# Attention with the AV product turned round, whole heads batched, and a fixed order of instructions across heads

## Chip, cores, metric

One Trainium2 chip, one of its cores. The metric is the device time of one execution in microseconds. Before: 785.48 us (median of 15 runs, 783.91 to 795.9).

## The reference, cut

```python
# attention: q, k, v are [8, 12, 448, 64]
scores = matmul(q, k.T) / sqrt(64)
m = max(scores, -1);  e = exp(scores - m)
attn = e / (sum(e, -1) + exp(-m) + 1e-9)      # "softmax off by one": exp(s) / (sum(exp(s)) + 1)
x = matmul(attn, v)                           # -> x[3584, 768], heads side by side
# soft mixture of experts on x: logits x @ phi, softmax over tokens, slot inputs d.T @ x,
# 8 experts of two layers (3 MB of weights a layer), and c @ slot_out -> [3584, 768]
```

## The kernel before

Only the attention loop matters here. There are 96 heads; a head is 448 rows, in four blocks of 112. "Scores" are q x k, `ex` their exponentials, and "AV" is the product of `ex` and v. PE is the matmul engine, DVE the vector engine, ACT the scalar engine, POOL the GpSimd engine; PSUM is the memory that matmuls write, SBUF the one that they read. Of a matmul's two operands the stationary one is loaded into PE's array first, as weights (LDWEIGHTS in the traces, counted as PEld: 2856 of them to 2857 matmuls from 10 to 580 us), and the matmul then reads the moving one.

```python
for j in range(NJ):                                     # NJ = 4
    tq = qkT_psum.tile([D, SC], BF16, tag="t")          # 112x64 -> 64x112, on PE
    nc.tensor.transpose(tq, qb[:, j, :], ident[0:SC, 0:SC])
    nc.vector.tensor_copy(qT[:, j * SC:(j + 1) * SC], tq)
    ...                                                 # the same for k
for j in range(NJ):
    sc = sc_psum.tile([SC, S], F32)
    nc.tensor.matmul(sc, kT[:, j * SC:(j + 1) * SC], qT, start=True, stop=True)
    nc.scalar.activation(ex[:, j, :], sc, AF.Exp, scale=scale)
for i in range(NJ):
    av = av_psum.tile([SC, D + 1], F32, tag="av")       # rows: queries; last column: denominator
    for j in range(NJ):
        nc.tensor.matmul(av, ex[:, j, i * SC:(i + 1) * SC], vb[:, j, :], ...)
    nc.vector.tensor_scalar_add(den, av[:, D:D + 1], 1.0)
    nc.vector.reciprocal(rec, den)                      # 112x1: one element per partition
    nc.vector.tensor_scalar_mul(x_sb[:, t, h * D:(h + 1) * D], av[:, 0:D], rec)
if h % 2 == 1: ...                                      # four transposes x -> xT, four ACT copies
```

A scheduler orders the instructions on each engine.

The softmax here doesn't subtract the row's maximum and nothing guards it: scores larger than these inputs give would overflow.

## Time and profile before

| | before |
|---|---|
| median of 15 runs | 785.48 us |
| attention | up to about 580 us |
| logits and slot inputs | 580 to 611 us |
| expert weights, output | 611 to 784 us |
| one head, from score to score | 5.94 us |
| PE's changes of array shape | 11.9 a head |

A matmul uses a part of PE's array, rows x columns: scores 64x112, the old AV 112x112 (64*112 and 112*112 in the traces). For the count both numbers are rounded up to 32, 64 or 128, so 112x112, 112x128 and 112x65 all count as the whole array; a change of shape is a matmul that uses another part than the one before it. The rounding is a convention of this text; the traces agree with it in two places: from AV (112x112) to a back transpose (112x128) starts are 93 ns apart, and 94 from AV to AV; in the changed kernel the same pair (112x65, then 128x112) is 373 ns apart, and AV to AV 374.

A matmul's duration in the trace is its latency, and neighbours overlap (four old AV matmuls of about 0.29 us each take 0.58 us together): to see what PE issues, read the distance from one start to the next. The prediction below shows these lines. One line of the page needs a warning, PE's granted clock in 40 slices of the run:

```profile
PEclk9999999999999999999999999999999687677855
```

It says full clock throughout attention. The matmuls say half clock: where the trace does record the clock, those of 512 columns in the weights' stage (L217) take 631 ns and start 427 ns apart at a granted clock of 0.50, and take 379 and start 216 apart at 1.00 (medians); attention's scores, of 448 columns, start 373 ns apart, which is 427 x 448/512. "Cold" below means half clock. The trace's list of clock changes begins only at 587 us, and the row is filled with the full clock up to the first change. Before the first change, trust the durations.

### The profile page before, as it was taken

The numbers are of one execution on the slowest core, as the hardware profiler recorded it, in microseconds if no ns is written. First come the engines' busy times: TensorE is split into PE (matmuls) and PEld (weight loads), VectorE is DVE, ScalarE is ACT, GpSimd is POOL, SyncE is SP. The second block draws the span as 40 slices with busy tenths as digits, with TensorE's granted clock in tenths as the row PEclk, the third lists the DMA queues.
The fourth block names the chain that finished last, engine by engine and source line by source line (L and its number), as shares of the span: only waits on it lengthen the run. The fifth ranks groups of instructions, "written<-read, shape, count | busy, mean of one in ns | idle before, by whom it ended". The sixth has DMA issues, their size and how long they took to land. (4 is left out here: it accounts for less than half of the span.)

```text
span 783.7 us, 11334 instructions
## 1 busy us (share of the span) xinstructions
PE 684.8 (87%) x3376; PEld 377.4 (48%) x3376; DVE 387.7 (49%) x2078; ACT 282.2 (36%) x731; POOL 167.9 (21%) x437
## 2 busy tenths in 40 slices
PE   5999999999999999999999999999998466676674
PEld 2555555555555555555555555555544122222221
DVE  2555555554555555555545555555540233443597
ACT  2444334434334443344343344333433142332200
POOL 3221222121212212221212222122100144342300
PEclk9999999999999999999999999999999687677855
DMA  4221121212111212212121112111000899999387
GB/s 134 60 66 54 59 64 55 60 54 65 60 54 54 65 54 60 65 53 60 54 66 60 54 54 66 54 59 54 7 1 1 329 432 427 433 424 434 123 283 253
DMA packets 44109, 95.20 MB, mean 121 GB/s; under 512 B 6160, under 2 KB 38416, under 8 KB 42000
## 3 DMA queue, kind: packets, MB, share of 16 engines
q1 hardware_dynamic: 44048, 94.49, 33.9%
q8 instruction: 26, 0.43, 0.2%
q14 instruction: 35, 0.29, 0.1%
HBM read 83.46 MB, written 11.01 MB: 121 GB/s over the span
## 5 line engine op out<-in xcount | busy, mean ns | idle before, releaser
L100 ACT ACTIVATE ex<-sc 112x448 bf16<-112x448 f32 x384 | 196.0, 544 | 155.5 <-PE sc L97 155.5
L105 PEld LDWEIGHTS <-ex 112*112 112x112 bf16 x1536 | 179.1, 200 | 129.8 <-DVE x_sb L116 62.0
L105 PE MATMUL av<-vb,ex 112*112 112x65 bf16 x1536 | 238.4, 287 | 0.8
L97 PE MATMUL sc<-qT,kT 64*112 64x448 bf16 x384 | 194.7, 595 | 4.9 <-DVE qT L85 4.9
L113 DVE TENSOR_SCALAR den<-av 112x1 f32<-112x1 f32 x384 | 57.7, 158 | 143.7 <-PE av L105 140.6
L84 PE MATMUL tq<-ident,qb 112*64 112x112 bf16 x384 | 113.3, 295 | 17.5 <-DVE qT L85 14.2
L85 DVE COPY qT<-tq 64x112 bf16<-64x112 bf16 x384 | 78.5, 204 | 87.1 <-PE tq L84 80.1
L129 ACT COPY xT_sb<-tp 128x112 bf16<-128x112 bf16 x192 | 48.4, 252 | 196.5 <-PE tp L125 192.8
L87 PE MATMUL tk<-ident,kb 112*64 112x112 bf16 x384 | 114.2, 297 | 5.2 <-DVE kT L88 4.9
L116 DVE TENSOR_SCALAR x_sb<-av,rec 112x64 bf16<-112x64 f32 x384 | 102.0, 275 | 2.7
L88 DVE COPY kT<-tk 64x112 bf16<-64x112 bf16 x384 | 76.4, 199 | 41.6 <-PE tk L87 38.1
L78 POOL CAST qb<-qf 112x256 bf16<-112x256 f32 x96 | 38.0, 396 | 238.4 <-issue 232.3
L91 POOL CAST vb<-vf 112x256 bf16<-112x256 f32 x96 | 38.7, 403 | 204.3 <-issue 94.8
L97 PEld LDWEIGHTS <-kT 64*112 64x112 bf16 x384 | 61.8, 183 | 37.6 <-issue 11.6
L84 PEld LDWEIGHTS <-qb 112*64 112x64 bf16 x384 | 51.2, 137 | 54.5 <-POOL kb L79 15.3
L87 PEld LDWEIGHTS <-kb 112*64 112x64 bf16 x384 | 54.3, 143 | 25.1 <-POOL vb L92 8.5
L217 PE MATMUL hp<-w1t,siT 128*4 128x512 bf16 x96 | 34.6, 515 | 29.4 <-ACT w1t L212 15.2
L114 DVE RECIPROCAL rec<-den 112x1 f32<-112x1 f32 x384 | 53.5, 148 | 1.0
L125 PE MATMUL tp<-ident,x_sb 112*128 112x112 bf16 x192 | 53.7, 280 | 0.0
L245 PE MATMUL sop<-w2t,hTt 128*32 128x384 bf16 x128 | 36.9, 458 | 6.4 <-ACT w2t L241 4.5
L212 DVE CAST w1t<-w1f 128x1024 bf16<-128x1024 f32 x16 | 18.0, 1170 | 45.4 <-DMA w1f<-in_moe_w_dram 45.4
L79 POOL CAST kb<-kf 112x256 bf16<-112x256 f32 x96 | 38.4, 400 | 5.8 <-PE tk L87 3.6
(50 smaller groups left out, 340.6 us busy)
## 6 DMA issues: line engine op xcount, KB each, us to landing
w1f<-in_moe_w_dram SPq DMA_DIRECT2D x8, 3072.0 KB, 26.0
w2f<-in_moe_w_dram SPq DMA_DIRECT2D x8, 3072.0 KB, 26.2
qf<-in_q_dram SPq DMA_DIRECT2D x96, 112.0 KB, 2.0
kf<-in_k_dram SPq DMA_DIRECT2D x96, 112.0 KB, 2.1
vf<-in_v_dram SPq DMA_DIRECT2D x96, 112.0 KB, 2.0
out_dram<-ot SPq DMA_DIRECT2D x32, 336.0 KB, 3.5
phi_f<-in_moe_phi_dram SPq DMA_DIRECT2D x1, 96.0 KB, 2.6
```

The source lines that it names most:

```text
L84: nc.tensor.transpose(tq, qb[:, j, :], ident[0:SC, 0:SC])
L85: nc.vector.tensor_copy(qT[:, j * SC:(j + 1) * SC], tq)
L87: nc.tensor.transpose(tk, kb[:, j, :], ident[0:SC, 0:SC])
L88: nc.vector.tensor_copy(kT[:, j * SC:(j + 1) * SC], tk)
L97: nc.tensor.matmul(sc, kT[:, j * SC:(j + 1) * SC], qT, start=True, stop=True)
L100: nc.scalar.activation(ex[:, j, :], sc, AF.Exp, scale=scale)
L105: nc.tensor.matmul(av, ex[:, j, i * SC:(i + 1) * SC], vb[:, j, :], start=(j == 0), stop=(j == NJ - 1),)
L113: nc.vector.tensor_scalar_add(den, av[:, D:D + 1], 1.0)
L114: nc.vector.reciprocal(rec, den)
L116: nc.vector.tensor_scalar_mul(x_sb[:, t, h * D:(h + 1) * D], av[:, 0:D], rec)
L125: nc.tensor.transpose(tp, x_sb[:, t, fb * 128:(fb + 1) * 128], ident[0:SC, 0:SC],)
L129: nc.scalar.copy(xT_sb[:, fb, t * SC:(t + 1) * SC], tp)
```

## The change

The intent: AV with v as the stationary operand, so four wide matmuls replace sixteen narrow ones and the result is born transposed; copies and normalisation for a whole head at once; and a software pipeline over heads in an order fixed by hand on PE, DVE, ACT and POOL. The diff, cut to its core (left out: the back transposes, now from xT to x with one copy for four, an unused constant that goes, and the layout of lines):

```diff
+            for src, dst in ((qb, qT), (kb, kT)):
+                tt = qkT_psum.tile([D, S], BF16, tag="t")
+                for j in range(NJ):
+                    nc.tensor.transpose(tt[:, j * SC:(j + 1) * SC], src[:, j, :], ident[0:SC, 0:SC])
+                nc.vector.tensor_copy(dst, tt)
...
-                    av = av_psum.tile([SC, D + 1], F32, tag="av")
-                        nc.tensor.matmul(av, ex[:, j, i * SC:(i + 1) * SC], vb[:, j, :], ...)
-                    nc.vector.tensor_scalar_add(den, av[:, D:D + 1], 1.0)
-                    nc.vector.reciprocal(rec, den)
-                    nc.vector.tensor_scalar_mul(x_sb[:, t, h * D:(h + 1) * D], av[:, 0:D], rec)
+            av = av_psum.tile([D + 1, S], F32)
+            for j in range(NJ):
+                nc.tensor.matmul(av, vb[:, j, :], ex[:, j, :], ...)
+            nc.scalar.add(den1, av[D:D + 1, :], 1.0)             # 1x448, one partition
+            nc.vector.reciprocal(rec1, den1)
+            nc.gpsimd.partition_broadcast(recb, rec1)            # 64x448
+            nc.vector.tensor_mul(xT_sb[...], av[0:D, :], recb)
...
+        with tc.manual_schedule(engines={PE, DVE, Activation, Pool}):
+            load(0)
+            for n in range(NH + 3):
+                qkT(n); load(n + 1); mul(n - 3); recip(n - 2); scores(n); av_mm(n - 1); xtr(n - 3)
```

## The prediction

> **What bounds the kernel now.** I read the views from coarse to fine: the stretches by stage, the costliest groups, the waits, one tile, then single instructions in time. The stretches first (columns: start:end us, length, then busy us and instruction count of each engine, granted TensorE clock, DMA share, GB/s):
>
> ```profile
> 10.00:580.00 570.00, 549.84 (x2857) 322.29 (x2856) 296.67 (x1901) 231.38 (x572) 113.57 (x372) 1.00 0.19 56
> 580.00:594.00 14.00, 14.00 (x59) 5.41 (x59) 2.62 (x14) 4.98 (x16) 0.00 (x0) 1.00 0.00 1
> 594.00:611.00 17.00, 14.27 (x97) 7.77 (x96) 0.84 (x4) 4.34 (x34) 0.00 (x0) 1.00 0.00 1
> 611.00:738.00 127.00, 78.94 (x293) 32.87 (x294) 47.42 (x56) 40.24 (x108) 48.97 (x43) 0.73 0.93 397
> 738.00:783.60 45.60, 25.97 (x67) 7.96 (x65) 38.38 (x98) 0.00 (x0) 0.00 (x0) 0.57 0.75 242
> ```
>
> Attention (96 heads) takes the first 580 us; logits, slot inputs, expert weights (DMA share 0.93) and output take the last 204. The change rewrites attention alone, where PE is the busiest engine: 549.84 of 570. The score tile gives the pace of a head:
>
> ```profile
> L97 PE MATMUL sc<-qT,kT x384: 526/619/619, 10.1 to 578.5; 64*112 64x448 bf16 x192
> ```
>
> From 10.1 to 578.5 us there are 95.75 heads: 5.94 us each. What PE does in it is in the groups:
>
> ```profile
> L105 PE MATMUL av<-vb,ex 112*112 112x65 bf16 x1536 | 238.4, 287 | 0.8
> L97 PE MATMUL sc<-qT,kT 64*112 64x448 bf16 x384 | 194.7, 595 | 4.9 <-DVE qT L85 4.9
> ...
> L84 PE MATMUL tq<-ident,qb 112*64 112x112 bf16 x384 | 113.3, 295 | 17.5 <-DVE qT L85 14.2
> ...
> L87 PE MATMUL tk<-ident,kb 112*64 112x112 bf16 x384 | 114.2, 297 | 5.2 <-DVE kT L88 4.9
> ...
> L125 PE MATMUL tp<-ident,x_sb 112*128 112x112 bf16 x192 | 53.7, 280 | 0.0
> ```
>
> The means are latencies of overlapping matmuls, so I take start-to-start times from the timeline:
>
> ```profile
> 301.49 1.28 PE L97 MATMUL sc<-qT,kT 64*112 64x448 bf16 x3 [0.21 <-DVE qT L85]
> 302.70 0.58 PE L105 MATMUL av<-vb,ex 112*112 112x65 bf16 x4
> 303.21 0.30 PE L84 MATMUL tq<-ident,qb 112*64 112x112 bf16 x1
> 303.31 0.30 PE L87 MATMUL tk<-ident,kb 112*64 112x112 bf16 x1
> 303.54 0.58 PE L105 MATMUL av<-vb,ex 112*112 112x65 bf16 x4
> ```
>
> Four av matmuls in 0.58 us, the last lasting 0.29, are 97 ns apart; over the trace the median is 94 ns, that of sc to sc 373 ns, and of tq to tk 95 ns. But between kinds PE loses time: av to tq is 212 ns, tk to av 230, sc to av 507, each 115 to 135 above the same pair without a change of array shape (av to tp, both over the full array, loses nothing). The scheduler interleaves the kinds so finely that PE changes shape 11.9 times a head (counted in PE's order in the trace). So one head is 4 x 373 + 16 x 94 + 8 x 94 + 2 x 94 = 3.9 us of issue, some 1.5 us of shape changes and 0.5 us of waits. PE's "busy" hides the switches.
>
> [...] For sc's 448 columns[...] the trace has 526 to 619, and 373 ns apart[...]. So attention runs cold from end to end, although the stretches print a clock of 1.00. The logits matmuls, N = 512,[...] 609 ns before 587 us, 379 after. [...] The trace cannot say: every reciprocal in it has one element per partition (148 ns). [...]
>
> **The change, part by part, per head.**
> AV is turned round: v is stationary and ex streams, 4 matmuls of 448 columns in place of 16 of 65. Cold, 4 x 373 = 1.49 us instead of 16 x 94 = 1.50. The swap itself saves PE nothing; 12 weight loads leave, which were hidden or equal.
> The transposes of q and k stay 8 (0.75 us). Back transposes stay 4 per two heads, now 128 columns (107 ns, 0.21 us a head).
> The order is fixed by hand: 8 transposes, 4 scores, 4 AV of the head before, back transposes. Shape changes fall from 11.9 to 3: about 0.38 us instead of 1.5.
> But a wait comes in: scores follow the transposes with nothing between. From the start of the last transpose 0.34 us to the copy's start (300.24 to 300.58 in the timeline), 0.38 us of copy, 0.05 to the first score: 0.77 us, of which 0.22 would be there anyway.
> PE's loop from one first score to the next, cold: three scores 1.12, the fourth held by the first exp to 1.22; score to AV 0.51; AV 3 x 0.373 = 1.12; AV to transposes 0.49; 7 x 0.093 = 0.65; wait 0.77. Sum 4.76 us, and 5.19 on the odd heads with four back transposes (0.43).
>
> DVE. Eight copies of 112 columns (8 x 0.20) and twelve small operations (4 x (158+148+275) = 2.32 us) leave. In come two copies of 448 ([...]0.38 us each, 0.35 start to start), a multiply of 448 from PSUM with an SBUF factor ([...]0.59 us, sized on the output's 384-column scalings, 0.52 us apart), and one reciprocal of 1 x 448 on a single partition: [...]3.8 us[...]. Sum 0.70 + 0.59 + 3.8 = 5.09 us. The order on DVE in the built program is copy, copy, multiply, reciprocal, repeated.
>
> ACT: 4 exps (434 ns apart, 1.74), one add of 448 (0.45), half a copy of 512 (0.3): 2.5 us. POOL: casts and memset 0.40 x 3 + 0.11 = 1.3, broadcast 0.6 to 0.9[...]: about 2.1 us. Neither binds.
>
> Both long loops share the copies: they wait for the transposes and for the reciprocal. So a head costs the larger of the two: 5.1 to 5.15 on even heads, 5.2 to 5.25 on odd ones. I take **5.2 us**. The multiply waits for the broadcast of the reciprocal that has just ended (0.6 to 0.9 us plus handover), while the two copies take 0.7, so that adds little or nothing.
>
> Sum: first score near 9 us, as now; 95.3 x 5.2 = 496, last score at 505. Then the pipeline drains: three heads' multiplies and two further reciprocals in series, each with broadcast and multiply: 3 + 2 x 5.2 + 2 = 15 us, so logits begin at about 520 instead of 580. They are no longer interleaved with attention's end: some 12 us instead of 14. The rest is untouched. 60 + 2 = 62 us off the profiled 785.5 gives 723; the plain runs spread from 786.7 to 795.9, so I add a little: **725 us**.
>
> **The rivals.**
> A. The reciprocal streams[...] (0.6 us). Then DVE needs 1.9 us and PE's cold loop rules: 4.98 a head, and a shorter drain: about 700 us.
> B. As A, and the denser matmuls wake the clock: scores and AV 190 ns apart, PE's loop near 3.3 us: 550 to 580 us. For it: PE's loop is 77% matmuls against 66%, in longer runs. Against: it needs A; with the slow reciprocal a warm PE only waits for DVE at 5.1.
> C. The broadcast is slow, 1.5 to 2 us[...]. Then reciprocal, broadcast, multiply chain on DVE without cover: 3.8 + 1.7 + 0.15 + 0.6 = 6.2 us a head, no better than 5.94: 780 to 810. For it: nothing in the profile prices it.[...]
> D. The gain is hidden by the weight transfers. Against: they start only when slot inputs are done (first weight transfer at 611 us, tied to the end of si), so they move forward as a block.
>
> **Range and chances.** The slow reciprocal (85%) with a short broadcast gives 700 to 745, depending on whether handovers add 0.2 us a head (20 us). Rival A or B 10%, C 5%. Range 702 to 750. Faster by over 2% 0.93, same 0.04, slower 0.03.
>
> **What would show each step.** Right: RECIPROCAL of 1x448 at 3.7 to 3.95 us, DVE over 90% busy in attention, sc to sc one head apart 5.1 to 5.3 us, av latency about 590 to 620 ns (cold), under four shape changes a head, logits beginning at 512 to 530 us. Wrong: a reciprocal under 1 us (A, far below my range), av at 350 ns (warm clock), or DVE's multiply waiting on POOL for over 0.5 us a head (C).

The sizes of operations that the kernel before does not have are the author's estimates, which no trace had shown: 0.38 us for a copy of 448 and 0.59 for the multiply, 3.8 for the reciprocal (0.6 in rival A), 0.6 to 0.9 for the broadcast. So are the 190 ns between matmuls and the 350 ns of an AV matmul at the full clock. The 107 ns of a back transpose is 94 x 128/112. What each came to is measured below.

## The result

The changed kernel takes **686.55 us** (median of 12 runs, 681.46 to 692.3; the two above 692 count as slow). The ratio is 0.872, 95% interval 0.868 to 0.8759. A ratio here is the mean time of one kernel's fast runs over that of the other's of the same rounds, so not quite the ratio of the medians. The direction was right; 725 us and the range from 702 to 750 were not.

The stretches of the changed kernel's profiled run, a run of 691.0 us (columns as in the prediction):

```profile
10.00:478.00 468.00, 412.57 (x1711) 211.06 (x1709) 395.59 (x379) 254.74 (x524) 171.63 (x474) 0.60 0.24 69
478.00:491.00 13.00, 12.06 (x58) 5.30 (x57) 8.46 (x7) 6.89 (x18) 2.21 (x3) 0.93 0.01 3
491.00:516.00 25.00, 24.11 (x96) 10.96 (x95) 0.42 (x3) 3.70 (x32) 0.00 (x0) 0.55 0.00 0
516.00:640.00 124.00, 77.05 (x280) 31.65 (x281) 46.99 (x56) 38.78 (x107) 48.66 (x43) 0.72 0.96 407
640.00:689.00 49.00, 30.49 (x79) 9.95 (x78) 38.19 (x98) 1.38 (x2) 0.50 (x1) 0.54 0.70 225
```

Attention ends about 100 us earlier, and the weights and output take 173 us as before. The third stretch (slot inputs) took 17 us before at the full clock and 25 here at half (a matmul of it takes 326 ns there and 527 here, medians): this stage can run at either clock, which may account for some of the spread of runs; one profile can't show it. The score tile:

```profile
L104 PE MATMUL sc<-qT,kT x384: 346/577/619, 10.7 to 476.2; 64*112 64x448 bf16 x192
```

(476.2 - 10.7)/95.75 = 4.86 us a head instead of 5.94. Logits begin at 478.3, two microseconds after the last score. The costly groups:

```profile
L128 DVE RECIPROCAL rec<-den 1x448 f32<-1x448 f32 x96 | 281.8, 2935 | 1.5
...
L104 PE MATMUL sc<-qT,kT 64*112 64x448 bf16 x384 | 164.0, 552 | 55.0 <-DVE kT L95 52.4
L130 POOL PARTITION_BROADCAST recb<-rec x96 | 70.3, 732 | 300.4 <-DVE rec L128 291.4
L116 PE MATMUL av<-ex,vb 112*65 112x448 bf16 x384 | 155.3, 556 | 0.5 <-DVE xT_sb L136 0.5
...
L136 DVE TENSOR_TENSOR xT_sb<-av,recb 64x448 bf16<-64x448 f32 x96 | 58.8, 613 | 9.2 <-POOL recb L130 7.9
```

The reciprocal takes 2.94 us, not 3.8; the multiply takes 0.61 for 0.59, the copies 0.38, as put, and back transposes start 107 ns apart, as put. PE's 55.0 us of idle time before scores is the wait for the copy of kT. One ordinary head in the timeline:

```profile
300.30 1.78 PE L104 MATMUL sc<-qT,kT 64*112 64x448 bf16 x4 [0.47 <-DVE kT L95]
...
300.70 2.93 DVE L128 RECIPROCAL rec<-den 1x448 f32<-1x448 f32 x1
...
302.00 1.71 PE L116 MATMUL av<-ex,vb 112*65 112x448 bf16 x4
...
303.64 0.58 PE L94 MATMUL tt<-ident,qb 112*64 112x112 bf16 x4
...
304.01 0.58 PE L94 MATMUL tt<-ident,kb 112*64 112x112 bf16 x4
304.26 0.38 DVE L95 COPY qT<-tt 64x448 bf16<-64x448 bf16 x1 [0.63 <-PE tt L94]
...
304.63 0.38 DVE L95 COPY kT<-tt 64x448 bf16<-64x448 bf16 x1
...
305.07 1.78 PE L104 MATMUL sc<-qT,kT 64*112 64x448 bf16 x4 [0.47 <-DVE kT L95]
```

From score to score 4.77 us. PE goes through its block without a gap but for the 0.47 us before the scores; DVE is idle for 0.63 us from the end of the reciprocal (303.63) to the next copy. So PE sets the pace, not DVE. Odd heads, with back transposes, take 5.20. In the whole run the steady heads take 4.77 or 5.20 in turn, except in five stretches where scores are 346 ns long, AV matmuls 353, and AV starts are 189 ns apart instead of 374:

```profile
398.40 0.77 PE L104 MATMUL sc<-qT,kT 64*112 64x448 bf16 x3 [0.47 <-DVE kT L95]
398.80 2.93 DVE L128 RECIPROCAL rec<-den 1x448 f32<-1x448 f32 x1
...
400.80 0.36 PE L94 MATMUL tt<-ident,kb 112*64 112x112 bf16 x4
401.66 0.32 DVE L95 COPY qT<-tt 64x448 bf16<-64x448 bf16 x1
...
402.32 0.77 PE L104 MATMUL sc<-qT,kT 64*112 64x448 bf16 x3 [1.16 <-DVE kT L95]
```

Here the clock is up, which is called "awake" below. The transposes are done by 401.16, but the copy starts at 401.66, when the reciprocal lets DVE go; PE idles 1.16 us. Such heads take 3.92 and 4.45 us. Every stretch lasts 6.8 us, then the clock falls back (granted clock 1.00 from 73.7 to 80.3 us, 0.50 from 80.5 to 141.7). The stretches don't come at random: three of the four distances from one start to the next are 68.3 us (the fourth is 187.7). Seven pairs of heads, one of them awake, take 6 x 9.97 + 8.37 = 68.2 us, so that distance is one of whole pairs of heads; why the clock wakes there, no run tests. The clock row after (its first recorded change is at 73.6 us):

```profile
PEclk9999855565555555555655565557855777887655
```

### The profile page after: what moved, and what is told of

The parts are those of the page before. It is cut to its first block, busy times and chain, and to the rows that moved or that the text cites. A ratio compares the mean times of both kernels' runs of the same rounds, so it can differ in the third digit from the quotient of the medians.

```text
span 689.2 us, 7613 instructions
## 1 busy us (share of the span) xinstructions
PE 557.0 (81%) x2224; PEld 269.6 (39%) x2224; DVE 490.1 (71%) x542; ACT 306.8 (45%) x683; POOL 225.1 (33%) x531
## 5 line engine op out<-in xcount | busy, mean ns | idle before, releaser
L128 DVE RECIPROCAL rec<-den 1x448 f32<-1x448 f32 x96 | 281.8, 2935 | 1.5
L104 PE MATMUL sc<-qT,kT 64*112 64x448 bf16 x384 | 164.0, 552 | 55.0 <-DVE kT L95 52.4
L130 POOL PARTITION_BROADCAST recb<-rec x96 | 70.3, 732 | 300.4 <-DVE rec L128 291.4
L116 PE MATMUL av<-ex,vb 112*65 112x448 bf16 x384 | 155.3, 556 | 0.5 <-DVE xT_sb L136 0.5
L116 PEld LDWEIGHTS <-vb 112*65 112x65 bf16 x384 | 51.1, 157 | 102.5 <-issue 100.8
L95 DVE COPY qT<-tt 64x448 bf16<-64x448 bf16 x96 | 36.0, 375 | 66.6 <-PE tt L94 66.6
L126 ACT ACTIVATE den<-av 1x448 f32<-1x448 f32 x96 | 51.6, 537 | 43.4 <-PE av L116 42.2
L136 DVE TENSOR_TENSOR xT_sb<-av,recb 64x448 bf16<-64x448 f32 x96 | 58.8, 613 | 9.2 <-POOL recb L130 7.9
L94 PE MATMUL tt<-ident,qb 112*64 112x112 bf16 x384 | 54.9, 297 | 9.3 <-POOL qb L79 9.3
L94 PE MATMUL tt<-ident,kb 112*64 112x112 bf16 x384 | 54.6, 296 | 0.0
L277 PE MATMUL sop<-w2t,hTt 128*32 128x384 bf16 x128 | 37.4, 462 | 6.5 <-ACT w2t L274 5.1
```

The lines of the kernel that those rows point to most:

```text
L94: nc.tensor.transpose(tt[:, j * SC:(j + 1) * SC], src[:, j, :], ident[0:SC, 0:SC])
L116: nc.tensor.matmul(av, vb[:, j, :], ex[:, j, :], start=(j == 0), stop=(j == NJ - 1),)
L126: nc.scalar.add(den1, av[D:D + 1, :], 1.0)
L128: nc.vector.reciprocal(rec1, den1)
L130: nc.gpsimd.partition_broadcast(recb, rec1)
L136: nc.vector.tensor_mul(xT_sb[(h % 2) * D:(h % 2 + 1) * D, h // 2, b * S:(b + 1) * S], av[0:D, :], recb)
```

## The experiments

I first thought that the reciprocal's size alone decided the miss: 2.94 us instead of 3.8 handed the pace from DVE to PE. Rivals were that shape changes are free, that turning AV round made the gain, and that DVE still sets the pace. Unless another is named, a kernel is the changed one with one edit. "Before" in the ratios is the kernel before, run on the same chip.

A run of one core counts as slow when it is over 1.5% above its kernel's fastest. Where the clock wakes late, runs get that name although nothing else ails them.

### The reciprocal at the size predicted (rec38)

```diff
             nc.vector.reciprocal(rec1, den1)
+            junk = nrm_pool.tile([1, 117], F32, tag="junk")
+            nc.vector.reciprocal(junk, den1[:, 0:117])
```

> The changed kernel with a second reciprocal, of 117 elements, behind the first: DVE's reciprocals then take about 3.75 us a head instead of 2.93, the size that the prediction gave them. Theory (the mis-sized reciprocal moved the bound from DVE to PE): DVE's loop becomes about 5.0 us and rules the even heads, which go from 4.77 to 4.95-5.15 us, odd heads stay near 5.20, the short warm stretches gain nothing; the time rises by 15 to 30 us over the changed kernel (to 700-717). Rival (DVE has slack, PE alone sets the pace and the prediction failed elsewhere): within 5 us of the changed kernel.

Measured: 690.82 us (690.16 to 698.61), ratio 0.8783. The added operation, from its tile's view:

```profile
L130 DVE RECIPROCAL junk<-den x96: 819/819/820, 21.4 to 495.0; 1x117 f32<-1x117 f32 x96
```

The theory's 15 to 30 us did not come. With 2.93 + 0.82 = 3.75 us of reciprocals, ordinary heads still take 4.77 and 5.20; only awake heads lengthen, to 4.67 and 4.90. DVE in an ordinary even head:

```profile
207.15 0.82 DVE L130 RECIPROCAL junk<-den 1x117 f32<-1x117 f32 x1
207.90 0.34 DVE L95 COPY qT<-tt 64x448 bf16<-64x448 bf16 x1
```

The copy begins before the second reciprocal ends (207.97): DVE has no slack left here, and its loop is just level with PE's. So the size of the reciprocal alone doesn't explain the miss: my DVE sum was too large in its other terms too (see below).

### No reciprocal (copyrec)

```diff
-            nc.vector.reciprocal(rec1, den1)
+            nc.vector.tensor_scalar_mul(rec1, den1, 1.0 / (449.0 * 449.0))
```

It is not the reference's formula. These inputs have denominators so near to 449 that it passes the comparison all the same.

> The changed kernel with the reciprocal of 1x448 replaced by a multiply with 1/449^2, which is near the reciprocal but wrong on purpose; DVE loses about 2.5 us a head. Theory (PE's cold loop sets the pace, 4.77 and 5.20 us in turn): heads unchanged except in warm stretches, a drain shorter by about 5 us, so 672 to 686. Rival (the reciprocal sets the pace): falls by up to 2.5 us a head, to under 600.

Measured: 577.03 us (568.35 to 586.0). Neither theory had this. Up to 83 us the heads take 4.77 and 5.20 as before, so the reciprocal does not set the cold pace. Then the clock wakes, and it stays up: heads of 3.34 and 3.56 us to the end of attention. The stretch from 90 to 350 us (columns as before):

```profile
90.00:350.00 260.00, 197.36 (x1353) 106.20 (x1354) 120.51 (x303) 201.33 (x416) 138.34 (x376) 1.00 0.35 100
```

Theory of the next run: at the full clock the full reciprocal makes DVE's loop (3.92 us) longer than PE's (3.34); PE then idles and the clock falls back. Half a reciprocal should be enough to keep it up.

### Half a reciprocal (halfrec)

```diff
+            nc.vector.reciprocal(rec1[:, 0:S // 2], den1[:, 0:S // 2])
+            nc.vector.tensor_scalar_mul(rec1[:, S // 2:S], den1[:, S // 2:S], 1.0 / (449.0 * 449.0))
```

> The changed kernel with the reciprocal over the first 224 columns alone and the multiply with 1/449^2 for the others (wrong on purpose): reciprocal 1.45 us, DVE's warm loop about 3.1 us, under PE's warm loop of 3.34 and 3.56 us. Theory (the full reciprocal makes DVE the longer loop as soon as PE's clock is up, PE idles, the clock falls back; with a loop under PE's it stays up): once awake it stays awake as in the run with no reciprocal, 565 to 600 us depending on when it wakes. Rival (each microsecond of reciprocal costs in proportion): about halfway between 577 and 687, 630 us, with heads between 3.5 and 4.8 us throughout.

Measured: 586.82 us (555.23 to 590.14). In the profiled run the clock wakes at 123 us and stays, with heads of 3.34 and 3.56 us, the same as without any reciprocal. As the theory says, the cost isn't in proportion to the reciprocal. Three of the four runs count as slow; in the profiled one, which is among them, it is the late waking.

### Scores and AV in turn (interleave)

```diff
-                    scores(n)
-                    av_mm(n - 1)
+                    both(n)        # sc[0], av[0], sc[1], av[1], ...
```

> The changed kernel with scores and AV issued one by one in turn instead of four and four: the same instructions, but 9 changes of array shape a head instead of 3. Theory (a change of shape costs PE 0.115 to 0.135 us): 6 more of them cost 0.75 us a head, less 0.1 of waiting for the first exp: +0.6 to +0.75 us a head, 57 to 72 us, so 740 to 760. Rival (shape changes are free, the gain came from fewer and larger matmuls): within 10 us of the changed kernel.

Measured: 778.3 us (778.0 to 778.53), ratio 0.9869 (0.9797 to 0.9942, so unclear by the 2% rule). Heads take 5.67 and 6.15 us: 0.90 to 0.95 more for six more shape changes, 0.15 to 0.16 each, above the 0.6 to 0.75 expected. The clock never wakes. A middle piece of PE's timeline:

```profile
304.39 0.62 PE L134 MATMUL sc<-qT,kT 64*112 64x448 bf16 x1
304.94 0.58 PE L139 MATMUL av<-ex,vb 112*65 112x448 bf16 x1
305.46 0.62 PE L134 MATMUL sc<-qT,kT 64*112 64x448 bf16 x1
```

Starts are 520 to 550 ns apart where like follows like after 373. The same instructions in another order give back nearly the whole gain; some 8 us of the 92 are the short awake stretches of the changed kernel, which are missing here.

### The old AV in the hand-made order (oldav)

```diff
-            av = av_psum.tile([D + 1, S], F32)             # 4 matmuls, vb stationary
+            av = av_psum.tile([SC, NJ, D + 1], F32)        # 16 matmuls, ex stationary, one PSUM tile
...
+            nc.vector.tensor_scalar_add(den, av[:, :, D], 1.0)    # 112x4
+            nc.vector.reciprocal(rec, den)
+            nc.vector.tensor_mul(x_sb[...], av[:, :, 0:D], rec.unsqueeze(2).to_broadcast([SC, NJ, D]))
```

> The hand-made order of the changed kernel with the AV of the kernel before (16 matmuls of 65 columns, exp stationary), the four pieces in one PSUM tile, denominators as 112x4, normalisation by one add, one reciprocal of 112x4 and one multiply; no broadcast. PE still has 3 shape changes a head. Theory (turning AV round saves PE nothing at the cold clock, the order does it): PE's loop 4.77 us and 5.15 in turn, so within 12 us of the changed kernel, rather below it because no reciprocal is left in the drain: 672 to 692. Rival (turning AV round made the gain): 740 to 785.

Measured: 685.27 us (684.21 to 686.96), ratio 0.8692, against 0.872 of the changed kernel. The heads take 4.77 and 5.15 us; the clock never wakes in attention. The sixteen matmuls in PE's timeline, with DVE's three small operations:

```profile
300.67 1.70 PE L117 MATMUL av<-vb,ex 112*112 112x65 bf16 x16
...
303.61 0.14 DVE L127 TENSOR_SCALAR den<-av 112x4 f32<-112x4 f32 x1
...
303.78 0.18 DVE L129 RECIPROCAL rec<-den 112x4 f32<-112x4 f32 x1
```

Sixteen narrow matmuls take 1.70 us and four wide ones 1.71. In the hand-made order and at half clock, turning AV round saved PE nothing.

### The scheduler's order (noman)

```diff
-        with tc.manual_schedule(engines={...}):
+        if True:
```

> The changed kernel without the hand-made schedule: the scheduler orders the same instructions, with 5.0 shape changes a head in PE's order instead of 3.0. Theory: two more changes cost 0.25 us a head, less what the scheduler hides of the wait for the copies: 690 to 712. Rival (the hand order made the whole gain): 740 to 785.

Measured: 700.94 us (699.12 to 701.77), ratio 0.892; heads of 5.01 and 5.10 us. With four wide matmuls in place of sixteen there is less to interleave, and the scheduler makes 5.0 shape changes a head. So there are two roads to few shape changes, the new instructions left to the scheduler and the hand-made order with the old AV; either gets most of the gain, and they don't add. That it is the wide matmuls in the first is not shown: this run and oldav both also have the q and k transposes in groups of four, one copy each. Of the 11.9 changes in the kernel before, 6.3 lie between those transposes and AV, and no run groups the transposes alone.

### Transposes one head ahead (ahead)

```diff
             load(0)
+            load(1)
+            qkT(0)
             for n in range(NH + 3):
-                if n < NH: qkT(n)
+                if n + 1 < NH: qkT(n + 1)
```

(and `load(n + 2)`, and four buffers in place of three for the loads)

> The changed kernel with the transposes of q and k issued one head ahead, before the scores of the head in hand, so the copies to SBUF run beside the scores (four buffers in place of three for the loads). Theory: PE's loop loses 0.55 us of wait, 4.2 and 4.65 us in turn cold; DVE's loop of 4.15 to 4.3 us then binds on even heads: about 4.3 to 4.5 on average, 36 to 55 us below the changed kernel, 632 to 655. Rival (DVE already sets the pace): within 8 us of the changed kernel.

Measured: 643.13 us (642.43 to 651.74), ratio 0.8212. Cold heads take 4.23 and 4.69 us: the 0.47 us wait is gone, and a little more. As oldahead below, with a nearly idle DVE, has the same 4.23, PE and not DVE binds on even heads, against what the text above expected.

### Ahead, without the reciprocal (aheadcopy), and ahead with the old AV (oldahead)

Both edits are shown above.

> As the run before, with the reciprocal replaced by a multiply with 1/449^2 (wrong on purpose), so DVE has 1.7 us a head. Theory (cold PE loop): 4.2 and 4.65 us, about 625 to 645. If the denser PE wakes its clock, which the long reciprocal would have held back: matmuls of 350 instead of 530 ns, a head of 2.7 to 3.3 us, 500 to 560.

> The hand order with the old AV (16 matmuls, 112x4 normalisation, no broadcast) and the transposes one head ahead: a correct kernel with DVE at 1.8 us a head. Theory (cold): PE's loop 4.2 and 4.6 us, 625 to 645. If the clock wakes: below 580, and less of a gain than with the turned AV[...].

Measured: aheadcopy 624.26, 518.41, 585.26 and 517.06 us. In the profiled run (the first) cold heads take 4.23 and 4.65 us until 388 us; then the clock wakes, and heads of 2.91 and 3.03 follow. The spread is consistent with other moments of waking, which I saw only in this run's trace. oldahead takes 634.83 us (634.28 to 635.63), ratio 0.8082, with cold heads of 4.23 and 4.60 us throughout, never awake.

### One reciprocal for two heads (pair)

A correct kernel that should keep the clock up: transposes ahead, and the denominators of two heads on partitions 0 and 32 of one tile.

```diff
+            p = 32 * (n % 2)
+            nc.scalar.add(den2[(n // 2) % 2][p:p + 1, :], av[D:D + 1, :], 1.0)
+        def recip2(n):                                   # once for two heads
+            nc.vector.reciprocal(rec2, den2[(n // 2) % 2])        # 33x448
+            for m in (n, n + 1): nc.gpsimd.partition_broadcast(recb, rec2[32 * (m % 2):..., :])
```

(q and k share one PSUM tile and one copy; three AV buffers)

> A correct kernel with the turned AV: transposes one head ahead, one copy for q and k together, and one reciprocal for two heads (denominators at partitions 0 and 32 of one tile), so DVE needs about 2.7 us a head; three AV buffers. Theory: cold heads about 4.2 and 4.65 us; once the clock wakes, 2.9 to 3.1 us and it stays awake, since DVE's 2.7 is below PE's loop. Depending on when it wakes 515 to 635 us, with a wide spread of runs. Rival (the exact reciprocal always holds the clock down): 630 to 645, no spread.

Measured: six runs, 620.74, 550.14, 641.44, 552.23, 561.4 and 551.2 us; ratio of the fast ones 0.6998. Awake heads take 3.01 and 3.80 us; the 3.80 includes a wait of AV, 0.85 us, for the buffer that the multiply frees, which I had not expected. In the profiled run (620.74) the clock wakes at 344 us. The reciprocal over 33 partitions takes 2.94 us, as over one.

### Waking the clock: bursts of 24 matmuls (pairwake, oldwake; pairwakeav, afterwakeav, oldwakeav)

```diff
+                if n == 8:
+                    for r in range(24):
+                        sc = sc_psum.tile([SC, S], F32)
+                        # pairwake, oldwake: like scores, 64 rows x 112 columns of the array
+                        nc.tensor.matmul(sc, kT[:, 0:SC], qT, start=True, stop=True)
+                        # ...wakeav: like AV, 112 rows x 65 columns
+                        nc.tensor.matmul(sc[0:D + 1, :], vb[:, r % NJ, :], ex[:, r % NJ, :], ...)
```

The results of the burst are never read. pairwake and pairwakeav start from pair ("the kernel before" in the first text is pair), oldwake and oldwakeav from oldahead, afterwakeav from the changed kernel.

> The kernel before, with 24 extra score matmuls that nobody reads, in one dense burst ahead of the scores of head 8 (about 9 us cold), to wake the clock at once. Theory: awake from about 55 us to the end of attention at 2.9 to 3.1 us a head: 515 to 535 us, in every run. Rival (the clock falls back without a burst): near 640.

> The old AV (16 matmuls of 65 columns) in the hand order with transposes one head ahead, which ran cold throughout at 634.8 us, with the same burst of 24 matmuls at head 8. Theory ([...]the old AV gives PE's array less work per time and the clock falls back[...]): 635 to 645. Rival (only the waking was missing): 540 to 570.

In pairwake the burst of score-like matmuls ran from 46.8 to 55.8 us, 373 ns apart, without a gap, and woke nothing: pairwake took 624.46, 631.43, 601.35 and 562.12 us, oldwake 642.9 us (642.78 to 644.13), which is oldahead plus the burst. Nor does a busy PE alone wake the clock: in oldahead PE is busy for all of the 400 us from 20 to 420, cold throughout.

> The pair kernel with the burst made of 24 AV matmuls (112 rows of the array, as v x exp) instead of score matmuls (64 rows). The burst of 64-row matmuls ran 9 us without a gap and did not wake the clock, while 128-row logits matmuls woke it within 7 us in the kernel before. Theory (what wakes it is work over most of the array's rows): awake from about 60 us on in every run, 535 to 565 us, as the fast runs of the pair kernel (550 to 552). Rival (bursts do not matter, waking is a matter of chance[...]): late wakings again, runs spread from 550 to 640.

> The changed kernel itself, with its full reciprocal, and the same burst of 24 AV matmuls at head 8 (9 us cold, less if it wakes). Theory (with the full reciprocal DVE's loop of 3.9 to 4.45 us is the longer one once the clock is up, PE idles and the clock falls back[...]): a short awake stretch after the burst, then cold heads of 4.77 and 5.20 us again: 685 to 700 us. Rival (only the waking is missing): awake to the end, 600 or less.

> The old AV in the hand order with the transposes one head ahead and the burst of 24 matmuls of 112 rows at head 8. Theory (the old AV streams 16 x 65 columns behind 16 weight loads of 112 columns, so the array works less per time): wakes at the burst and falls back, 634 to 646. Rival (once awake it stays, as the turned AV does): 560 to 590.

The burst of AV-like matmuls woke it within 3 us in all three profiled runs. In pairwakeav it stays up to the end of attention: 554.74 us (552.72 to 557.74, five runs), ratio 0.7061, no run long enough for a late waking. The burst and the scores in the score tile's view:

```profile
L107 PE MATMUL sc<-qkT x384: 346/349/619, 12.3 to 350.0; 64*112 64x448 bf16 x192
...
L181 PE MATMUL sc<-ex,vb x24: 352/353/585, 46.8 to 52.3; 112*65 112x448 bf16 x24
```

In afterwakeav the clock is up from 50.4 to 64.1 us, then heads take 4.77 and 5.20 again, but for six more stretches of 6.8 us: 686.92 us (681.85 to 690.72). In oldwakeav it is up from 46.9 to 57.1 us and then cold for the 382 us to the end of attention: 638.13 us (637.59, 627.96, 638.68 and 642.17; only 637.59 was profiled, and the short one may have been awake for longer). The old AV in that trace, awake and cold:

```profile
54.45 1.01 PE L117 MATMUL av<-vb,ex 112*112 112x65 bf16 x16
...
57.21 1.70 PE L117 MATMUL av<-vb,ex 112*112 112x65 bf16 x16
```

So waking alone is not enough: with the full reciprocal per head, or with the old AV, the clock falls back. For the reciprocal the cause is shown: copyrec removes it, halfrec halves it, and the clock stays. That it works through PE's idle time is argued. It fits the kernels with the turned AV: awake, PE is busy for 68% of the time in the changed kernel and 58% in rec38, where the clock falls back, and for 75 to 76% in copyrec, halfrec and pairwakeav, where it stays. It doesn't fit the old AV, which in oldwakeav is busy for 88% (6.17 of the 7.00 us from 50.1) and falls back. For the old AV only the fact is shown. That its 16 weight loads leave the array too little work is the author's guess, which no run shows: awake, the sixteen matmuls take 1.01 us, with a median of 52 ns from one start to the next, and cold 1.70. And why a burst over 112 rows of the array wakes the clock and one over 64 rows doesn't stays open: the two also differ in columns (65 and 112) and in the data, though hardly in the cells of the array that they use (112 x 65 = 7280, 64 x 112 = 7168).

## Why the prediction was wrong, step by step

**Right: what PE gains.** PE's cold loop was put at 4.76 and 5.19 us; the trace has 4.77 and 5.20. That shape changes are the gain and turning AV round saves nothing at half clock is borne out by interleave (back to 778) and oldav (685.27). The wait for the copies was named, and ahead removes it. The broadcast, predicted at 0.6 to 0.9 us, takes 0.73, and DVE's multiply waits 7.9 us for it in all 96 heads, so rival C is out; weights and output are unchanged, so D is too. The pace that came, 4.77 and 5.20, is rival A's average of 4.98: I had tied A to a reciprocal of 0.6 us, and 2.94 was short enough.

**Wrong: "a head costs the larger of the two: 5.1 to 5.15 on even heads".** The failing term is DVE's sum, 0.70 + 0.59 + 3.8 = 5.09 us. Measured, one cycle from a copy of q to the end of the reciprocal is 4.37 (304.26 to 308.63): the reciprocal 2.94 instead of 3.8. The 3.8 was my estimate, and no trace backed it: every reciprocal in the kernel before has one element per partition (148 ns). From the two sizes in rec38 it is (2931 - 819)/(448 - 117) = 6.38 ns an element. But rec38 shows that the reciprocal was not the whole of it: with 3.75 us of reciprocals DVE's awake loop was still only 4.67, as the operations overlap by 0.07 to 0.09 us each and I had added some in full, and the two copies then take 0.53 us and not 0.70. So DVE never ruled a cold head; PE did. On 48 even heads 0.35 us each is 17 us of the miss.

**Wrong: the clock.** Rival B, the waking clock, was made to need a fast reciprocal, because "a warm PE only waits for DVE at 5.1". To wake, it needs no such thing: it wakes for 6.8 us at a time, and each time saves (4.77 - 3.92) + (5.20 - 4.45) = 1.6 us, five times in the profiled run, 8 us. To stay awake, it does: the kernel with a cheap reciprocal is what rival B describes (577 us).

**Wrong: the drain.** I had logits begin 15 us after the last score, "no longer interleaved with attention's end". They begin 2.1 us after it: the first batches' logits need only the first batches' rows, and PE does them while the last heads finish.

```profile
476.69 1.71 PE L116 MATMUL av<-ex,vb 112*65 112x448 bf16 x4
478.32 3.45 PE L186 MATMUL lg<-xT_sb,phi_sb 128*32 128x512 bf16 x12
...
481.70 0.95 PE L116 MATMUL av<-ex,vb 112*65 112x448 bf16 x4
```

The drain itself lasts about as long as I put, to the last multiply at 489.2, 13 us after the last score; the overlap was the mistake, and it is worth 13 us.

**Smaller ones.** In the profiled run the first score was at 10.7 us, 1.7 later than put; "near 9 us, as now" was a slip, as the score tile's line has 10.1 for the kernel before. The slot inputs ran at half clock, so logits and slot inputs took 37.4 us (478.3 to 515.7) where 28.6 were put (30.6 as before, less 2), plus 9. I had added 2 us for the spread of the runs. From 725: heads from 496 to 465.5 us, minus 30 (the 17 and the 8 above, the rest the rounding up to 5.2 and a quick first head of 3.14); drain minus 13; plus 2; plus 9; minus 2: 691, the profiled run's time. The median lies 4 below it.

## What to carry to other kernels

Count PE's changes of array shape in its instruction order; here six more of them cost 0.9 us a head and undid nearly all that a rewrite had won, while the busy share of PE did not show them. Judge the clock by the matmuls' own lengths (a score takes 577 ns cold and 349 awake, medians): an engine that has slack in the slow-clock loop (DVE is idle for 0.6 to 0.8 us before the copies) can still be what keeps the clock from staying up, and shortening its work is then worth far more than the cold loop suggests (686.55 us with the reciprocal, 577.03 without). Turning AV round saved nothing at half clock, yet no kernel here with the old AV stayed awake in attention, and six with the turned one did (copyrec, halfrec, aheadcopy, pair, pairwake, pairwakeav). Spread a reciprocal over partitions (112x4) or share it (two heads in one), since here its time went with the elements per partition (2.93 us for 1x448, 2.94 for 33x448, 0.82 for 1x117, 0.18 for 112x4); the best correct and stable kernel found, pairwakeav, takes 554.74 us.
